# Half of x transposed by DMA, and a stricter order on VectorE, in a gated spectral and dense layer with its gradients

## The chip, the core and the metric

The kernel runs on one core of a Trainium2 chip. The metric is the device time of one launch in microseconds (us); the numbers below are medians of several runs, and the profile is one execution of the same program recorded by the hardware profiler.

## The reference

The forward pass mixes two branches with a gate, row by row. Branch A is a two-dimensional real Fourier transform of x, a product with a complex filter, and the transform back. Branch B is a dense layer with a squared ReLU between two products. The kernel returns the output and the gradients of A_x, A_w_r, A_w_i, w1, b1, w2, b2 and gate_w for a given grad_out.

```python
# S = 2048 rows, D = 1024, F = 3584, all bfloat16
x = A_x
g = sigmoid((x * gate_w).sum(-1, keepdims=True))
a = irfft2(rfft2(x) * (w_r + 1j * w_i))
h = relu(x @ w1 + b1); b = (h * h) @ w2 + b2
out = g * a + (1 - g) * b
# outputs: out, and the vjp of it for (A_x, A_w_r, A_w_i, B_w1, B_b1, B_w2, B_b2, gate_w)
```

Both branches take x = A_x; the input B_x is not used.

## The kernel before

The program has one main stream of TensorE work and one side stream. The main stream has four stages: the products of the dense layer forward and back (`mlp_in`), the gradient of w2 and then of w1 (`mlp_grads`, with blocks multiplied by a scheme of seven products instead of eight, which needs sums and differences of operands on VectorE), and the output and the gradient of x (`mlp_out`). The side stream is the Fourier branch; `spread` draws units of it between the units of the main stream, in proportion to the weight that each main unit yields.

The products need x and the scaled gradient with their columns on the partitions: xT and dbT. Both are made by TensorE from tiles of 128 rows. A tile takes eight 128 x 128 transposes into one of two PSUM buffers, and one copy to SBUF:

```python
def turn_tile(dst, i, src, copy, tie=None):
    pt = tps.tile([P, DC, P], BF16, name="pt", tag="tr", bufs=2)
    for b in range(DC):                                   # DC = 8
        later["turned"] = nc.tensor.transpose(pt[:, b, :], src[:, b * P : (b + 1) * P], identb[:])
        after(later["turned"], tie, mybir.DependencyClass.NoSync)
    copy(out=dst[:, :, of_tile(i)], in_=pt[:])

def weigh(i, src):                                        # row sum of x * gate_w, for the gate
    unused = f1.tile([P, 2, H], FDT, name="uv", tag="uv", bufs=2)
    weighed = nc.vector.tensor_tensor_reduce(... in0=src[:], in1=gwb[:], ..., accum_out=gsum[:, i : i + 1])
    after(weighed, later.get("b1"), mybir.DependencyClass.NoSync)

def gate(i0):                                             # gate of four tiles, then the gradient's rows scaled
    c_ = slice(i0, i0 + 4)
    nc.scalar.activation(omg[:, c_], gsum[:, c_], ACT.Sigmoid, scale=-1.0)
    nc.scalar.activation(gcol[:, c_], gsum[:, c_], ACT.Sigmoid)
    for i in range(i0, i0 + 4):
        later["scaled"] = nc.vector.tensor_scalar(out=dbn[:, i, :], in0=dbn[:, i, :], scalar1=omg[:, i : i + 1], ...)
```

`after(a, b, NoSync)` only fixes that a stands after b; it adds no semaphore between engines. The program is ordered by a scheduler within such bounds. `queued` ties each load to the one before it, so that the loads stand in one order on SyncE's queue:

```python
def turn_x(i):
    src = rows.pop(i)
    weigh(i, src)
    turn_tile(xT, i, src, nc.vector.tensor_copy if i == 1 else nc.scalar.copy, ...)

def turn_grad(i):
    turn_tile(dbT, i, dbn[:, i, :], nc.vector.tensor_copy, later["product"])

# ... (start: loads, tiles 0 to 3 turned and weighed, gate(0), rows_of_grad(1))
rows_of_x(2); rows_of_grad(2); rows_of_x(3); rows_of_grad(3)      # loads of four tiles each
before = {1: [4], 2: [5], 3: [6, 7], **{u: [u - 4] for u in range(12, 20)}}
grads_before = {**{u: [u - 4] for u in range(4, 12)}, **{u: [u - 12] for u in range(20, 28)}}
for u in range(32):
    for i in before.get(u, ()):
        turn_x(i)
    for i in grads_before.get(u, ()):
        turn_grad(i)
    next(units)                                           # eight matmuls of 128 x 512
    if u in (3, 15, 19):
        gate({3: 4, 15: 8, 19: 12}[u])
    if u == 17:
        for n in range(3):
            xs[n] = source(n, x_perm)                     # rows for the Fourier side
        stage = first_stage_of_x()
    if u > 19 and u % 2:
        next(stage)
```

Of these 32 units, 0 to 7 multiply xT's tiles 0 to 7 with w1 (results ph), 8 to 15 multiply dbT's tiles 0 to 7 with the transposed w2 (results pd); 16 to 23 and 24 to 31 do the same with the tiles 8 to 15. Within each eight, the first four units use the first four of those tiles. The transposed w2 (w2T) comes from DMAs that transpose (`turned`), two of 256 rows x 1024 for each group; units 8 to 15 need the first group.

A block of the gradient of w1 runs in steps: p1 and p2 (no sums needed), p4 of the block before, p6, p3 of the block before, p5, p7. p5 needs the sum 1 of its group, p6 sum 2, p7 sum 3, p4 sum 4. Each group serves two blocks. The additions (`add`) take a result from PSUM (pV) and a kept one:

```python
# class Turned(Block), for the gradient of w1
def add(self, t_, h, kept):
    turn["DVE"] = super().add(t_, h, kept)
    return turn["DVE"]

# mlp_grads, at the switch from the gradient of w2 to that of w1 (cut)
c.p1(); yield each
c.p2(); yield each
sums_of_x(3, tie=c.first)
b.p5()
sums_of_group(FG, 4, 3)
fetch(FG + 2, 0); yield each
b.p6(); yield each
# ... c.p5, c.p6 with sums_of_x(4), b.p7
c.p7()
sums_of_group(FG + 1, 1, 2, tie=c.added); yield each
b.p4(); yield each
b.p3(); yield each
for k in range(NB // 2 + 2, NB):
    g, second = divmod(k, 2)
    b = Turned(k)
    b.p1(); yield each
    # ... p2, a.p4 (and sums_of_group(g, 3, 4) for the first block of a group), p6, a.p3, p5
    b.p7()
    if second and g + 1 < len(jobs):
        sums_of_group(g + 1, 1, 2, tie=b.added)
    yield each
```

`in_turn(ins, "DVE")` sets an instruction after the last one recorded in turn["DVE"]; the folds of the Fourier side's last stage use it already.

Of the kernel before, what the change touches and what calls it, by code (L numbers as in the profile page):

```python
# [14 lines left out]
ALU = mybir.AluOpType  # L15
# [125 lines left out]
def kernel(  # L141
# [22 lines left out]
    nc = tc.nc  # L164
# [6 lines left out]
    g = Geo(S, D, F)  # L171
    S2, DC, FC = g.S2, g.DC, g.FC
    R1, R2 = g.R1, g.R2
    NT = S // P
    Q, H, LW, W1 = D // 4, D // 2, g.Df + 1, g.Df
    FGW, FG, FGC = g.FGW, g.FG, g.FGC
# [4 lines left out]
    turned = lambda out, in_: nc.sync.dma_start(out=out, in_=in_, transpose=True)  # L181
    ld, st = nc.sync.dma_start, nc.gpsimd.dma_start
    V, mm = nc.vector.tensor_tensor, nc.tensor.matmul
# [5 lines left out]
    x_perm = xf.rearrange("(p t) d -> t p d", t=S2)  # L189
# [41 lines left out]
    def of_tile(i):  # L231
        return slice(P * i, P * (i + 1))

    def after(ins, earlier, wait=mybir.DependencyClass.Sync):

        if earlier is not None:
            info = mybir.DependencyInfo(wait, mybir.DependencyReason.DATA)
            tc.add_manual_dep(ins.ins, earlier.ins.name, info, reason="paced")


    turn = {"PE": None, "DVE": None, "ACT": None, "copy": None}
# [5 lines left out]
    def in_turn(ins, eng):  # L247
        after(ins, turn[eng], mybir.DependencyClass.NoSync)
# [366 lines left out]
    def rows_of_w2(t_, fc, half, tie=None):  # L615
        src = B_w2[fc * P : (fc + 4) * P, half * H : (half + 1) * H]
        after(ld(out=t_[:, fc : fc + 4, :], in_=src.rearrange("(q p) e -> p q e", p=P)), tie)
# [4 lines left out]
    xT = xT_p.tile([P, DC, S], BF16, name="xT", tag="xT")  # L622
    dbT = xT_p.tile([P, DC, S], BF16, name="dbT", tag="dbT")

    later = {}
# [5 lines left out]
    def queued(ins):  # L631
        after(ins, later.get("row"), mybir.DependencyClass.NoSync)
        later["row"] = ins
# [9 lines left out]
    def turn_tile(dst, i, src, copy, tie=None):  # L643

        pt = tps.tile([P, DC, P], BF16, name="pt", tag="tr", bufs=2)
        for b in range(DC):
            later["turned"] = nc.tensor.transpose(pt[:, b, :], src[:, b * P : (b + 1) * P], identb[:])
            after(later["turned"], tie, mybir.DependencyClass.NoSync)
        copy(out=dst[:, :, of_tile(i)], in_=pt[:])  # L649

    def vectors(vrow):
        vps = tps.tile([P, FC], BF16, name="vps", tag="tr", bufs=2)
# [8 lines left out]
        nc.scalar.copy(out=gwb[:], in_=pb[:])  # L661
        return gwb

    def weigh(i, src):
        unused = f1.tile([P, 2, H], FDT, name="uv", tag="uv", bufs=2)
        weighed = nc.vector.tensor_tensor_reduce(
            out=unused[:].rearrange("p a b -> p (a b)"), in0=src[:], in1=gwb[:], scale=1.0, scalar=0.0,
            op0=ALU.mult, op1=ALU.add, accum_out=gsum[:, i : i + 1],
        )
        after(weighed, later.get("b1"), mybir.DependencyClass.NoSync)  # L670

    def gate(i0):

        c_ = slice(i0, i0 + 4)
        nc.scalar.activation(omg[:, c_], gsum[:, c_], ACT.Sigmoid, scale=-1.0)
        nc.scalar.activation(gcol[:, c_], gsum[:, c_], ACT.Sigmoid)
        for i in range(i0, i0 + 4):
            later["scaled"] = nc.vector.tensor_scalar(out=dbn[:, i, :], in0=dbn[:, i, :], scalar1=omg[:, i : i + 1], scalar2=None, op0=ALU.mult)

    def first_stage_of_x():  # L680
        f, ft = {0: folds(f1, xs[0], later["last"])}, {}
        for i in range(NT + 1):
            if i + 3 < NT:
                xs[i + 3] = source(i + 3, x_perm, later["last"])
            if i < NT:
                ft[i] = row_stage(f1, f[i], kf[:], later["last"])
                yield
            if i > 0:
                first_columns(f1, cf, 0, i - 1, ft[i - 1], later["last"])
            if i + 1 < NT:  # L690
                f[i + 1] = folds(f1, xs[i + 1], later["last"])
            yield
# [149 lines left out]
    def mlp_grads():  # L842
# [12 lines left out]
        jobs = [(h2T_scr, fg) for fg in range(FG)] + [(dhT_scr, fg) for fg in range(FG)]  # L855
# [34 lines left out]
        T_, S_, blk = {}, {}, {}  # L890
# [32 lines left out]
        class Block:  # L923
# [7 lines left out]
            def operands(self):  # L931
                (a11, a12), (_, a22) = quads(grp[self.g], FH)
                self.A = {"11": a11, "12": a12, "22": a22, **S_.setdefault(self.g, {})}
                self.S, self.T = S_[self.g], T_
                self.a11, self.a12, self.a22 = a11, a12, a22
                self.b11, self.b21, self.b22 = b11, b21, b22
# [19 lines left out]
            def add(self, t_, h, kept):  # L956
                return V(out=self.side(t_, h), in0=self.flat(self.V[:]), in1=self.flat(kept[:]), op=ALU.add)
# [36 lines left out]
        class Turned(Block):  # L994

            def operands(self):
                (self.a11, self.a12), (_, self.a22) = quads(xr, H)
                (self.b11, self.b21), (_, self.b22) = quads(grp[self.g], FH)
                self.S, self.T = X_, T_[self.g]

            flat = staticmethod(lambda ap: ap.rearrange("p (j f) -> p j f", j=2))

# [3 lines left out]
                return t_  # L1006

            def add(self, t_, h, kept):
                turn["DVE"] = super().add(t_, h, kept)
                return turn["DVE"]  # L1010

            def side(self, t_, h):
                return t_.rearrange("p (j h f) -> p h j f", j=2, h=2)[:, h]
# [18 lines left out]
        X_ = {}  # L1032
# [20 lines left out]
        def sums_of_group(g, *which, tie=None):  # L1053
            (g11, g21), (g12, g22) = quads(grp[g], FH)
            made = T_.setdefault(g, {})
            for n in which:
                if n == 3:
                    made[3] = fp16(g12)
                else:
                    tag = {1: "S3", 2: "S2", 4: "S4"}[n]  # L1060
                    made[n] = sb.tile([P, KH, FH], FP16, name=f"G{n}", tag=tag, bufs=2 if n == 1 else 1)[:]
                x, y = {
                    1: lambda: (g12, g11),
                    2: lambda: (g22, made[1]),
                    3: lambda: (g22, g12),
                    4: lambda: (g21, made[2]),
                }[n]()
                after(V(out=made[n], in0=x, in1=y, op=ALU.subtract), tie, mybir.DependencyClass.NoSync)

        NB = 2 * len(jobs)  # L1070
        each, none = 0.5, 1e-6
        for k in range(2):
            blk[k] = Block(k)
        fetch(1, 0, 1)
# [35 lines left out]
        for k in range(2, NB // 2):  # L1110
            a = blk.pop(k - 1)
            g, second = divmod(k, 2)
            b = blk[k] = Block(k)
# [35 lines left out]
        b, c = (Turned(NB // 2 + n) for n in range(2))  # L1149
# [10 lines left out]
        fetch(FG + 1, 1)  # L1160
        yield each
        c.p1()
        yield each
        c.p2()
        yield each
        sums_of_x(3, tie=c.first)
        b.p5()
        sums_of_group(FG, 4, 3)
        fetch(FG + 2, 0)
        yield each  # L1170
        b.p6()
        yield each
        c.p5()
        yield each
        c.p6()
        sums_of_x(4)
        yield each
        b.p7()
        yield each
        c.p7()  # L1180
        sums_of_group(FG + 1, 1, 2, tie=c.added)
        yield each
        b.p4()
        yield each
# [3 lines left out]
        for k in range(NB // 2 + 2, NB):  # L1188
            g, second = divmod(k, 2)
            b = Turned(k)  # L1190
            b.p1()
            yield each
            b.p2()
            if second:
                fetch(g + 2, 0)
            yield each
            a.p4()
            if not second:
                sums_of_group(g, 3, 4)
            yield each  # L1200
            b.p6()
            yield each
            a.p3()
            if not second:
                fetch(g + 1, 1)
            yield each
            b.p5()
            yield each
            b.p7()
            if second and g + 1 < len(jobs):  # L1210
                sums_of_group(g + 1, 1, 2, tie=b.added)
            yield each
            n = k - NB // 2 - 2
            if n < FC // 4:
                rows_of_w2(later["w2L"], 4 * n, 0, b.added)
            a = b
# [456 lines left out]
    rows = {}  # L1673

    def rows_of_x(k):
        for i in range(4 * k, 4 * (k + 1)):
            rows[i] = source(i, x_perm, None, "xsrc")

    def rows_of_grad(k):
        for i in range(4 * k, 4 * (k + 1)):  # L1680
            queued(ld(out=dbn[:, i, :], in_=go_perm[i]))

    def turn_x(i):
        src = rows.pop(i)
        weigh(i, src)
        turn_tile(xT, i, src, nc.vector.tensor_copy if i == 1 else nc.scalar.copy, later["gate_row"] if i == 2 else later.get("product"))

    def turn_grad(i):
        turn_tile(dbT, i, dbn[:, i, :], nc.vector.tensor_copy, later["product"])
# [32 lines left out]
    gate(0)  # L1722
    next(units)
    rows_of_grad(1)
    rows_of_x(2)
    rows_of_grad(2)
    rows_of_x(3)
    rows_of_grad(3)
    for t_, n in ((kf, "kf"), (flip, "flip"), (sel, "sel"), (cf, "cf")):
        after(st(out=t_[:], in_=cten[n].ap()), later["scaled"])  # L1730
    stage = None
# [2 lines left out]
# [3 lines that stand above are left out]
        for i in grads_before.get(u, ()):  # L1737
            turn_grad(i)
        next(units)
        if u in (3, 15, 19):  # L1740
            gate({3: 4, 15: 8, 19: 12}[u])
        if u == 17:
            for n in range(3):
                xs[n] = source(n, x_perm)
# [3 lines that stand above are left out]
# [97 lines left out]
```

## Time and profile before

Three runs took 1213.85, 1214.64 and 1214.91 us; the median is 1214.64. The profiled execution spans 1213.9 us at a mean granted TensorE clock of 0.997. Its stages, by start of their first work:

| stage | from us | what fills it |
|---|---|---|
| start, and 32 units with transposes between | 0 | TensorE, loads |
| rest of the products forward and back | 86 | TensorE |
| gradient of w2 | 466 | TensorE, VectorE |
| gradient of w1 | 641 | TensorE, VectorE |
| output, gradient of x | 845 | TensorE |

Of TensorE's work, the lines that the change speaks of, in the page's form (line engine op, out<-in, xcount | busy us, mean ns of one | idle us before, releaser):

```profile
L647 PE MATMUL pt<-identb,dbn 128*128 128x128 bf16 x128 | 10.2, 223 | 2.4 <-DVE dbT L649 2.4
L647 PE MATMUL pt<-identb,xsrc 128*128 128x128 bf16 x128 | 10.1, 231 | 0.0
```

The busy time of a group counts overlapping instructions once, so 128 transposes of 231 ns each fill 10.1 us. Names used below: xsrc are rows of x, dbn rows of grad_out (scaled in place), ph and pd results of the two products, wlo and whi outputs of a gradient block, G the sums of a group, pki and rf the Fourier side's last stage and its folded input. PE is TensorE, DVE VectorE, ACT ScalarE, SP SyncE.

### The profile page before, as it was taken

How to read it: one execution, taken by the hardware profiler on the slowest of the kernel's cores; microseconds unless marked ns; L12 is line 12 of the kernel's file. 1: busy time of each engine (PE TensorE's matmuls, PEld its weight loads, DVE VectorE, ACT ScalarE, POOL GpSimd, SP SyncE). 2: the span in 40 equal slices, each digit the busy share in tenths (PEclk: the TensorE clock that was granted, in tenths of full speed). 3: DMA queues.
4: the chain of work that ended last, by engine and by line, in shares of the span. 5: the costliest groups of instructions: out<-in, count | busy, mean ns of one | idle time of the engine just before them, and what ended most of it. 6: DMA issues, size and time to landing. Idle time of an engine off the chain costs nothing. (4 is left out here: it accounts for less than half of the span.)

```text
span 1213.9 us, 19997 instructions
## 1 busy us (share of the span) xinstructions
PE 1192.4 (98%) x7213; PEld 651.6 (54%) x7213; DVE 844.2 (70%) x1841; ACT 624.5 (51%) x1130; POOL 364.4 (30%) x587
## 2 busy tenths in 40 slices
PE   8999999999999999999999999999999999999998
PEld 4555545544444444444447888888444444444444
DVE  6756646676879887877789746765488866966464
ACT  5447757855877863444444435554455523233322
POOL 1024424423455551433333444444232100000000
PEclk9999999999999999999999999999999999999999
DMA  9647576575858598999999699867885699975551
GB/s 291 195 148 182 164 203 194 151 173 178 203 173 210 183 227 168 184 212 222 226 200 189 159 227 223 209 165 204 256 234 158 195 209 238 236 215 177 154 154 35
DMA packets 332656, 234.43 MB, mean 193 GB/s; under 512 B 197789, under 2 KB 291515, under 8 KB 332556
## 3 DMA queue, kind: packets, MB, share of 16 engines
q1 hardware_dynamic: 301104, 141.98, 52.1%
q0 software_dynamic: 30224, 90.61, 23.5%
q8 instruction: 56, 0.92, 0.3%
q10 hardware_dynamic: 1228, 0.57, 0.2%
q14 instruction: 44, 0.36, 0.1%
HBM read 107.24 MB, written 81.81 MB: 156 GB/s over the span
## 5 line engine op out<-in xcount | busy, mean ns | idle before, releaser
L746 PE MATMUL ph<-xT,w1g 128*128 128x512 bf16 x896 | 218.8, 379 | 1.6 <-ACT xT L649 1.6
L754 PE MATMUL pd<-dbT,w2T 128*128 128x512 bf16 x896 | 213.6, 381 | 1.9 <-DVE dbT L649 1.9
L754 PEld LDWEIGHTS <-w2T 128*128 128x128 bf16 x896 | 87.2, 98 | 104.7 <-issue 3.4
L746 PEld LDWEIGHTS <-w1g 128*128 128x128 bf16 x896 | 85.1, 98 | 93.0 <-DMA w1g<-in_B_w_dram 1.5
L758 DVE SCALAR_TENSOR_TENSOR dhT<-pd,rT 128x512 bf16<-128x512 f32 x108 | 74.2, 687 | 77.3 <-PE pd L754 62.8
L747 ACT ACTIVATE rT<-ph,b1col 128x512 bf16<-128x512 f32 x108 | 74.5, 690 | 47.2 <-PE ph L746 46.9
L1020 PEld LDWEIGHTS <-res 128*128 128x128 bf16 (+1 forms) x896 | 86.7, 98 | 13.8 <-issue 2.8
L1372 PEld LDWEIGHTS <-dS 128*128 128x128 f16 x588 | 57.1, 98 | 66.8 <-issue 1.2
L226 POOL DMA_DIRECT2D r<-y_scr x96 | 58.3, 612 | 108.4 <-ACT re L553 42.4
L419 ACT CAST x<-px 64x512 f16<-64x512 f32 x128 | 74.2, 579 | 28.5 <-PE px L416 27.4
L226 POOL DMA_DIRECT2D z_scr<-u x96 | 58.6, 617 | 92.0 <-ACT u L294 48.0
L1020 PEld LDWEIGHTS <-X 128*128 128x128 f16 x672 | 64.9, 98 | 8.7 <-issue 0.9
L748 ACT ACTIVATE h2T<-rT 128x512 bf16<-128x512 bf16 x108 | 68.0, 630 | 2.2
L1372 PEld LDWEIGHTS <-odd 128*128 128x128 bf16 (+1 forms) x392 | 38.1, 98 | 44.9
L1372 PEld LDWEIGHTS <-even 128*128 128x128 bf16 (+1 forms) x392 | 38.0, 98 | 44.4
L456 POOL DMA_DIRECT2D y_scr<-pc x64 | 36.0, 564 | 69.0 <-DVE pc L453 66.2
L946 PEld LDWEIGHTS <-S 128*128 128x128 f16 x336 | 32.8, 98 | 39.7 <-DVE S L920 0.3
L394 POOL COPY w<-wn 128x512 bf16<-128x512 bf16 x32 | 23.1, 721 | 84.3 <-DVE tt L427 66.3
L568 ACT CAST rt<-pki 128x1024 f16<-128x1024 f32 x32 | 32.4, 1012 | 28.5 <-PE pki L566 28.2
L1394 DVE TENSOR_TENSOR cu<-pV,u 128x512 f16<-128x512 f32 x27 | 18.6, 689 | 40.8 <-PE pV L1372 35.1
L1345 POOL DMA_DIRECT2D out_dram<-gxo x14 | 7.6, 541 | 130.7 <-DVE gxo L1344 130.7
L1372 PE MATMUL pX<-wT,dS 128*128 128x512 f16 x196 | 44.8, 379 | 0.5 <-DVE dS L1368 0.5
(275 smaller groups left out, 2483.3 us busy)
## 6 DMA issues: line engine op xcount, KB each, us to landing
h2T_scr<-h2T POOLq DMA_DIRECT2D x28, 512.0 KB, 4.1
dhT_scr<-dhT POOLq DMA_DIRECT2D x28, 512.0 KB, 5.7
z<-z_scr SPq DMA_DIRECT2D x64, 128.0 KB, 3.0
y_scr<-pc POOLq DMA_DIRECT2D x64, 128.0 KB, 4.5
ax_scr<-yo POOLq DMA_DIRECT2D x32, 256.0 KB, 4.1
out_dram<-whi POOLq DMA_DIRECT2D x28, 256.0 KB, 4.4
out_dram<-wlo POOLq DMA_DIRECT2D x28, 256.0 KB, 4.4
even<-h2T_scr SPq DMA_DIRECT2D x8, 896.0 KB, 6.3
```

Source lines behind the costliest of these rows:

```text
L226: issue(out=a, in_=b) if stored else issue(out=b, in_=a)
L419: nc.scalar.copy(out=x[lanes[n], c, :, 0:HW], in_=px[lanes[c], n])
L456: st(out=y_scr[:][c, :, :, h].rearrange("r x t l -> (r x) t l"), in_=pc[:, n])
L568: nc.scalar.copy(out=rt[n][:], in_=pk[:])
L746: opened(mm(ph[:], lhsT=w1g[:, dc, fc % 2 * P : (fc % 2 + 1) * P], rhs=xT[:, dc, ss], start=(dc == 0), stop=(dc == DC - 1)), fc)
L747: nc.scalar.activation(rT[:], ph[:], ACT.Relu, bias=b1col[:, fc : fc + 1])
L748: nc.scalar.activation(h2T, rT[:], ACT.Square)
L754: opened(mm(pd[:], lhsT=w_[:, ec, fc % FGC * P : (fc % FGC + 1) * P], rhs=dbT[:, ec, ss], start=(ec == 0), stop=(ec == DC - 1),), fc)
L758: return STT(out=dhT, in0=pd[:], scalar=2.0, in1=rT[:], op0=ALU.mult, op1=ALU.mult, accum_out=gb1part[:, fc, sb : sb + 1],)
L946: self.mm = mm(acc[:], lhsT=lhs[:, t, c_], rhs=rhs[:, t, :], start=start and t == 0, stop=t == KH - 1, skip_group_check=True,)
L1020: ins = mm(acc[:, j * FH : (j + 1) * FH], lhsT=lhs[:, t, c_], rhs=rhs[:, t, :], start=start and first_ is None, stop=t == KH - 1, skip_gro ...
L1372: pe(mm(acc[:], lhsT=lhs[:, c, :], rhs=rhs[:, c, :], start=start and c == 0, stop=c == KH - 1, skip_group_check=True,))
```

## The change

The change has several parts. Tiles 8 to 15 of x are transposed by eight loads with a transpose, directly into xT, while their plain rows are still loaded for the row sums; TensorE's transposes and ScalarE's copies for them go. At the start the copies of transposes come first on VectorE: tile 3's copy moves to VectorE, the row sums 0 to 3 come after it, later row sums and the scaling of the gradient's rows stand behind the latest copy, and the scaling of rows 4 to 7 moves from unit 3 to unit 6. In the gradient of w1, sums of a group and additions stand in one order on VectorE, and the sums 1 and 2 come after the first chain of the group's own first block. At the switch five steps weigh 0.25 instead of 0.5, so that less of the side stream falls there.

```diff
-        copy(out=dst[:, :, of_tile(i)], in_=pt[:])
+        later["copied"] = copy(out=dst[:, :, of_tile(i)], in_=pt[:])
@@ weigh
-        after(weighed, later.get("b1"), mybir.DependencyClass.NoSync)
+        after(weighed, tie, mybir.DependencyClass.NoSync)
@@ gate
             later["scaled"] = nc.vector.tensor_scalar(out=dbn[:, i, :], ...)
+            after(later["scaled"], later["copied"], mybir.DependencyClass.NoSync)
@@ class Turned
-                self.S, self.T = X_, T_[self.g]
+                self.S, self.T = X_, T_.setdefault(self.g, {})
             def add(self, t_, h, kept):
-                turn["DVE"] = super().add(t_, h, kept)
-                return turn["DVE"]
+                ins = super().add(t_, h, kept)
+                in_turn(ins, "DVE")
+                turn["DVE"] = ins
+                return ins
@@ sums_of_group
-                after(V(out=made[n], in0=x, in1=y, op=ALU.subtract), tie, mybir.DependencyClass.NoSync)
+                ins = V(out=made[n], in0=x, in1=y, op=ALU.subtract)
+                after(ins, tie, mybir.DependencyClass.NoSync)
+                if g > FG:
+                    in_turn(ins, "DVE")
+                    turn["DVE"] = ins
@@ the switch
-        each, none = 0.5, 1e-6
+        each, slow, none = 0.5, 0.25, 1e-6
   (the yields after c.p1, c.p2, the fetch after b.p5, b.p6, c.p5: "yield slow" for "yield each";
    five such lines)
         c.p7()
-        sums_of_group(FG + 1, 1, 2, tie=c.added)
@@ the blocks after it
             b.p1()
+            if not second:
+                sums_of_group(g, 1, 2)
             yield each
   ...
             b.p7()
-            if second and g + 1 < len(jobs):
-                sums_of_group(g + 1, 1, 2, tie=b.added)
             yield each
@@ turn_x
-        src = rows.pop(i)
-        weigh(i, src)
-        turn_tile(xT, i, src, nc.vector.tensor_copy if i == 1 else nc.scalar.copy, ...)
+        if i >= NT // 2:
+            weigh(i, rows.pop(i), later["copied"])
+            return
+        turn_tile(xT, i, rows[i], nc.vector.tensor_copy if i in (1, 3) else nc.scalar.copy, ...)
+        if i >= 3:
+            for n in range(4 if i == 3 else 1):
+                weigh(n if i == 3 else i, rows.pop(n if i == 3 else i), later["copied"] if i == 3 else None)
@@ the loads
-    rows_of_x(2)
-    rows_of_grad(2)
-    rows_of_x(3)
-    rows_of_grad(3)
+    for k in (2, 3):
+        for i in range(4 * k, 4 * (k + 1)):
+            queued(turned(xT[:, :, of_tile(i)], x_perm[i]))
+        rows_of_x(k)
+        rows_of_grad(k)
@@ the units
-        if u in (3, 15, 19):
-            gate({3: 4, 15: 8, 19: 12}[u])
+        if u in (6, 15, 19):
+            gate({6: 4, 15: 8, 19: 12}[u])
```

More of the change, by code (lines that the diff above doesn't have):

```diff
@@ L662, in everywhere, with weigh @@
         return gwb
-    def weigh(i, src):
+    def weigh(i, src, tie):
         unused = f1.tile([P, 2, H], FDT, name="uv", tag="uv", bufs=2)
@@ L1162, in mlp_grads @@
         c.p1()
-        yield each
+        yield slow
         c.p2()
-        yield each
+        yield slow
         sums_of_x(3, tie=c.first)
@@ L1169, in mlp_grads @@
         fetch(FG + 2, 0)
-        yield each
+        yield slow
         b.p6()
-        yield each
+        yield slow
         c.p5()
-        yield each
+        yield slow
         c.p6()
@@ L1683, in turn_x @@
     def turn_x(i):
-        src = rows.pop(i)
-        weigh(i, src)
-        turn_tile(xT, i, src, nc.vector.tensor_copy if i == 1 else nc.scalar.copy, later["gate_row"] if i == 2 else later.get("product"))
+        if i >= NT // 2:
+            weigh(i, rows.pop(i), later["copied"])
+            return
+        turn_tile(xT, i, rows[i], nc.vector.tensor_copy if i in (1, 3) else nc.scalar.copy, later["gate_row"] if i == 2 else later.get("product"))
+        if i >= 3:
+            for n in range(4 if i == 3 else 1):
+                weigh(n if i == 3 else i, rows.pop(n if i == 3 else i), later["copied"] if i == 3 else None)
     def turn_grad(i):
```

## The prediction

> **What bounds the kernel now.** I read the engines' busy shares first, then the stretches of the span, then the waits of TensorE alone, and last the timeline around the two stretches in which TensorE idles and which the change touches.
>
> The page's first part gives busy us, share of the span and instructions:
>
> ```profile
> PE 1192.4 (98%) x7213; PEld 651.6 (54%) x7213; DVE 844.2 (70%) x1841; ACT 624.5 (51%) x1130; POOL 364.4 (30%) x587
> ```
>
> TensorE is busy for 1192.4 of 1213.9 us. So a gain can come from two sources only: TensorE work that disappears, and the 21.5 us in which TensorE is idle. A perfect removal of all idle time would be 1.8%. The stretches show where these 21.5 us lie (columns: length, busy us and count of PE, PEld, DVE, ACT, POOL, then granted clock, DMA share, GB/s):
>
> ```profile
> 25.00:37.00 12.00, 7.64 (x46) 3.94 (x44) 11.60 (x23) 2.82 (x6) 1.46 (x2) 0.86 1.05 387
> 37.00:52.00 15.00, 15.00 (x113) 8.50 (x111) 11.15 (x27) 4.35 (x6) 0.71 (x1) 1.00 0.32 121
> 650.00:676.00 26.00, 23.23 (x203) 19.61 (x201) 25.18 (x41) 12.11 (x23) 12.38 (x19) 1.00 0.78 170
> 735.00:845.00 110.00, 108.37 (x1100) 96.91 (x1099) 69.89 (x216) 60.29 (x111) 50.88 (x83) 1.00 0.80 196
> 870.00:950.00 80.00, 77.26 (x447) 37.41 (x446) 69.68 (x150) 43.34 (x70) 20.54 (x35) 1.00 0.68 193
> ```
>
> TensorE idles 12.00 - 7.64 = 4.4 us at 25 to 37 us, 2.8 us at the switch from the gradient of w2 to that of w1 (650 to 676), 1.6 us in the gradient of w1, and 2.7 us in the last stage, which the change does not touch. In the first two VectorE is full (11.60 of 12.00, 25.18 of 26.00). TensorE's list of waits names what ended its idle time:
>
> ```profile
> PE pt L647 <- DVE dbT L649: 2.4, 1, 2.4
> PE pV L1020 <- DVE wlo L957: 2.0, 1, 2.0
> PE pd L754 <- DVE dbT L649: 1.9, 1, 1.9
> ```
>
> All three are copies or additions of VectorE that had come late. The timeline of 23 to 33 us shows why (start, length, instruction):
>
> ```profile
> 23.45 1.08 DVE L678 TENSOR_SCALAR dbn<-dbn,omg 128x1024 bf16<-128x1024 bf16 x2 [2.35 <-DMA dbn<-in_grad_out_dram]
> ...
> 26.19 1.22 DVE L666 CUSTOM_DVE_ANT_0 uv<-xsrc,gwb 128x1024 f16<-128x1024 bf16 x1
> ...
> 27.34 0.68 DVE L649 COPY dbT<-pt 128x1024 bf16<-128x1024 bf16 x1
> ...
> 28.08 0.61 PE L647 MATMUL pt<-identb,dbn 128*128 128x128 bf16 x8 [2.42 <-DVE dbT L649]
> ...
> 32.81 3.29 PE L754 MATMUL pd<-dbT,w2T 128*128 128x512 bf16 x8 [1.95 <-DVE dbT L649]
> ```
>
> VectorE sits at the scaling of the gradient, which waits 2.35 us for a load, then does a row sum of x (1.22 us), and only then the copy of a finished transpose at 27.34. TensorE can't go on because both banks for transposes are full.
>
> [...] the copy at 27.34 stands behind a scaling that waits for data. [...] after two gaps of 2.42 and 1.95 us, with little between them, the granted clock was 0.86 over 25 to 37 us, and the eight products at 32.81 took 3.29 us where eight take 1.89. [...] at 15 to 20 us, when the transposing loads of w2T are nearly all that moves, the DMA share is 0.90 at 155 GB/s, and at 55 to 60 us, with such loads again, 218 GB/s at a share of 1.22. [...]
>
> **Part 1: half of x's transposes leave TensorE.** Eight tiles with eight transposes each go. A transpose's own duration (231 ns) overstates it, since they are pipelined. At 45.35 and 47.52 us two products of eight matmuls start 2.17 us apart with one tile's transposes between them; without any (645.46, 647.18, 648.91) they are 1.73 apart. So a tile costs 2.17 - 1.73 = 0.44 us, and eight cost 3.5 us, in a stretch where TensorE is full (37 to 70 us). ScalarE also loses eight copies of 1.01 us, off the path. **-3.5 us.**
>
> **Part 2: order on VectorE at the start.** Row sums 8 to 15 now stand behind the latest copy, so the one at 26.19 is no longer ahead of the copy of dbT. The second scaling moves from after unit 3 to after unit 6 and also stands behind a copy. What is to be won is the two gaps and the slow restart: 2.42 + 1.95 + (3.29 - 1.89) + 0.32 for the eight transposes after it (0.93 instead of 0.61) = 6.1 us. Rows 4 to 7 of the gradient land by about 25.4 either way, and without the row sum the fourth copy would be done near 27, about when unit 7 ends, so I take the whole 6.1. The copy of tile 3 on VectorE beside that of tile 2 on ScalarE would bring the first product from 9.99 to about 9.2, but tile 4's transposes wait for a load until 11.80 just after it, so I count only 0.3. **-6.4 us.**
>
> **Part 3: the new loads.** Two megabytes more have to come, at 155 to 218 GB/s: 9 to 13 us of DMA. Before, the DMA engines are full until 40 us (share 1.05 at 25 to 37) and almost idle from 40 to 52 us. So the last loads should land about 12 us later, near 52. There is a second limit. SyncE took 7.41 us to issue the two transposing loads of w2T, 1 MB in all. Eight of 256 KB would take 8 x 7.41 / 4 = 14.8 us, an estimate by size, and this queue issues in order. Its last gradient row, issued before by 33.2, would be issued near 48. Unit 16 started at 51.87 and unit 20 at 60.56; less 6.4 and four or eight tiles of 0.44 they start near 44 and 50.6. The half of xT that unit 16 needs is issued by about 29: safe. The other, for unit 20, is issued by about 41 and takes 5 to 11 us, as w2T's loads do: barely in time. The last scaling (unit 19, about 49) and the first rows of the Fourier side would wait on VectorE for loads that land at 52 to 55, with the copies of dbT behind them again. I set 2.3 us for this, between nothing and one more stall of the kind seen. **+2.3 us.**
>
> **Part 4: the switch.** Of 2.6 us (1.98 and 0.64), the larger wait is for the addition at 672.36, which stood behind three sums of group 8 (668.29, 669.76, 671.23, each 1.22) and two of the side stream. Two of these three now come after the next block's first chain, and all are in one order with the additions. Five steps draw half as much side work. Of the side stream some 64 units are left for a weight of 48 in this stage (counted in the code, with the 24 kept for the last one), so 5 x 0.25 x 64 / 48 = 1.7 units are put off, with 1.7 us or so of VectorE work each: 3 us less in a stretch of 26 where it is full. I take 2.2 of the 2.6. **-2.2 us.**
>
> **Part 5: one order in the gradient of w1.** 1.6 us of small waits lie there, mostly for folds of the Fourier side that stand behind sums of a group. The sums stay as long and come one chain later. I take **-0.4 us**. The side work put off, about two units, comes where the last stage already waits for VectorE: **+0.6 us.**
>
> Sum: -3.5 - 6.4 + 2.3 - 2.2 - 0.4 + 0.6 = -9.6, so 1214.64 - 9.6 = 1205.0 us. The stages between are full on TensorE (25.00 of 25.00 us in nearly every stretch from 275 to 650), so what is won early should reach the end.
>
> **Rivals.** (a) *The loads become the wait.* If the eight transposing loads run slower than by size, or w2T's next load is held behind them, xT comes late at unit 20 and TensorE stands for 5 to 10 us, with a slow restart on top: 1210 to 1218. For it speak 155 GB/s and the in-order queue; against it the empty stretch from 40 to 52 us. (b) *Only the transposes count.* The wait of VectorE at 23.45 is one for data, so the copies may just stand behind the scaling again, and the switch may find another sum in the way. Then only 3.5 us and a little of the rest remain: about 1210. For it speaks that two megabytes more are asked for; against it, that the needed gradient rows are issued before them. (c) *The strict order costs.* An addition that waits for a chain holds up the folds behind it, in each of twelve blocks: 0.3 us each would be +3.6 in place of -0.4: about 1209. (d) *All goes well:* no new wait and both stretches cleared, 1214.64 - 3.5 - 6.4 - 2.6 - 1.6, about 1200.
>
> **Range and chances.** From (d) and a little below to the mild end of (a): 1199 to 1213. A gain over 2% would need 24.3 us, more than all idle time: 0.01. A loss over 2% would need 24 us of new waits, several stalls of the first stretch: 0.02. Within 2%: 0.97.
>
> **What would show it.** Part 1: 64 transposes from xsrc instead of 128, and units 16 to 19 about 1.73 us apart. Part 2: no TensorE wait for dbT at 25 to 33 us, a clock of 1.00 there, and the first pd product near 27.5. Part 3: DMA busy at 40 to 52 us; a TensorE wait for xT, or for dbT behind a scaling, near 50 to 60 us would be (a). Part 4: no wait for wlo in the 26 us of the switch. Part 5: waits of pki for rf that shrink, or, under (c), grow. The prediction is wrong if the product stage ends less than 5 us earlier, or if what it wins is gone again at the end.

## The result, and the profile after

Four runs of the changed kernel have a median of 1207.67 us (1206.89 to 1208.85), against 1214.78 for the kernel before beside them. The ratio is 0.9938, 95% interval 0.9919 to 0.9957: 7.1 us faster by the medians. The profiled execution is the fastest of the four and spans 1205.1 us.

The three views shown before, for the changed kernel. The page's busy shares:

```profile
PE 1182.8 (98%) x7055; PEld 647.7 (54%) x7149; DVE 845.4 (70%) x1842; ACT 614.4 (51%) x1121; POOL 365.5 (30%) x587
```

The stretches (columns as before):

```profile
25.00:37.00 12.00, 11.95 (x86) 6.63 (x85) 7.75 (x17) 2.63 (x4) 1.54 (x2) 1.00 1.03 292
37.00:52.00 15.00, 14.89 (x75) 7.04 (x76) 10.97 (x25) 3.62 (x7) 1.42 (x2) 1.00 1.05 284
52.00:70.00 18.00, 13.40 (x92) 7.19 (x92) 11.38 (x29) 8.65 (x20) 1.42 (x2) 0.91 0.95 258
650.00:676.00 26.00, 26.00 (x232) 22.44 (x231) 24.41 (x39) 12.50 (x23) 10.26 (x18) 1.00 0.80 146
735.00:845.00 110.00, 108.35 (x1068) 93.71 (x1067) 69.21 (x211) 58.15 (x110) 49.71 (x80) 1.00 0.92 201
870.00:950.00 80.00, 77.50 (x452) 38.75 (x458) 71.13 (x153) 42.19 (x69) 21.62 (x37) 1.00 0.71 201
```

And TensorE's two longest waits (us in total, times, longest):

```profile
PE ph L747 <- ACT rT L748: 4.5, 1, 4.5
PE pki L566 <- DVE rf L558: 1.9, 4, 0.7
```

The stretch at 25 to 37 us is cured: TensorE is busy for 11.95 of 12.00 us instead of 7.64, at a clock of 1.00 instead of 0.86. So is the switch, 26.00 of 26.00. The DMA engines, at a share of 0.32 over 37 to 52 us before, are full (1.05). A new hole stands at 52 to 70 us, 13.40 of 18.00, with the clock at 0.91, and TensorE's longest wait is now one for ScalarE.

The timeline of that hole, TensorE, ScalarE and VectorE together (start, length, instruction):

```profile
48.85 1.23 DVE L666 CUSTOM_DVE_ANT_0 uv<-xsrc,gwb 128x1024 f16<-128x1024 bf16 x1 [3.83 <-DMA xsrc<-in_A_x_dram]
...
50.45 1.89 PE L747 MATMUL ph<-xT,w1g 128*128 128x512 bf16 x7
...
53.55 0.21 ACT L675 ACTIVATE omg<-gsum 128x4 f32<-128x4 f32 x1 [4.39 <-DVE gsum L666]
...
55.70 0.42 DVE L256 TENSOR_TENSOR uv<-src 128x512 f16<-128x512 bf16 x1 [2.19 <-DMA src<-in_A_x_dram]
...
56.50 0.20 ACT L263 COPY f<-uv 128x2 f16<-128x2 f16 x1 [2.13 <-DVE uv L257]
56.60 0.68 ACT L748 ACTIVATE rT<-ph,b1col 128x512 bf16<-128x512 f32 x1
...
57.33 3.57 PE L747 MATMUL ph<-xT,w1g 128*128 128x512 bf16 x8 [4.55 <-ACT rT L748]
...
57.97 0.68 DVE L649 COPY dbT<-pt 128x1024 bf16<-128x1024 bf16 x1
...
61.63 1.89 PE L747 MATMUL ph<-xT,w1g 128*128 128x512 bf16 x8
```

VectorE waits 3.83 us for the first late rows of x (tile 12), makes four row sums, then waits 2.19 us for the first rows of the Fourier side. ScalarE stands behind it twice: at the sigmoid of those sums (4.39 us), and at a copy of that fold (2.13). The relu of a finished product (56.60) comes after both, and TensorE's next product, unit 21 at 57.33, waits 4.55 us for it; the copy of dbT, at 57.97, is late as well. Unit 20 started at 50.45, and unit 22 at 61.63. Without the hole unit 22 would have started at 50.45 + 0.44 + 1.73 + 0.44 + 1.73 + 0.44 (two tiles of transposes and one set of eight from the Fourier side at 0.44 each, two products) = 55.2. So the hole costs 6.4 us: 4.6 of idle time, and the rest a slow restart, the eight products taking 3.57 us instead of 1.89.

To place the gains I read four landmarks in each trace: the first ph product after the 32 units, the first product of the gradient of w2, that of w1, and that of the last stage. Times in us from the span's start:

| kernel | after 32 units | gradient of w2 | gradient of w1 | last stage | span |
|---|---|---|---|---|---|
| before | 86.27 | 465.58 | 641.53 | 844.75 | 1213.9 |
| changed | 82.54 | 461.71 | 637.67 | 837.56 | 1205.1 |
| changed, all transposes on TensorE (run 1) | 80.34 | 459.61 | 635.57 | 835.15 | 1204.7 |
| before, transposing loads only (run 2) | 91.37 | 470.81 | 646.77 | 851.47 | 1220.2 |
| before, gradient of w1 only (run 3) | 86.09 | 465.26 | 641.21 | 840.79 | 1211.7 |
| late rows, four side units (run 4) | 75.69 | 457.25 | 638.21 | 838.98 | 1209.9 |
| late rows, six side units (run 5) | 77.13 | 456.31 | 632.26 | 831.85 | 1199.5 |
| before, VectorE order at the start only (run 6) | 80.21 | 459.49 | 635.44 | 838.91 | 1207.5 |
| changed, only tiles 8 to 11 by DMA (run 8) | 78.25 | 457.51 | 633.46 | 841.04 | 1209.3 |
| changed, transposes both ways (run 9) | 83.89 | 463.16 | 639.11 | 838.54 | 1208.4 |
| before, smaller weights only (run 10) | 85.16 | 464.33 | 640.29 | 841.79 | 1210.3 |
| before, order in the gradient of w1 only (run 11) | 85.22 | 464.40 | 640.35 | 840.77 | 1211.5 |

The change wins 3.7 us by the first landmark and keeps it to the third; the gradient of w1 takes 199.9 us instead of 203.2 and adds 3.3.

A landmark comes from one execution. Four traces have the start of the kernel before (before, runs 3, 10 and 11), and their first landmarks lie at 86.27, 86.09, 85.16 and 85.22 us. Run 10 shows where most of that comes from. It has the same two gaps as before, 2.46 and 1.95 us, but not the slow restart:

```profile
28.65 0.61 PE L647 MATMUL pt<-identb,dbn 128*128 128x128 bf16 x8 [2.46 <-DVE dbT L649]
...
33.38 1.89 PE L754 MATMUL pd<-dbT,w2T 128*128 128x512 bf16 x8 [1.95 <-DVE dbT L649]
```

The eight products take 1.89 us here and 3.29 in the trace of before. So a difference of about 1 us at the first landmark can be chance.

### The profile page after: what moved, and what is told of

Same layout as the page of the kernel before. It is cut to its first block, busy times and chain, and to the rows that moved or that the text cites. A ratio compares the mean times of both kernels' runs of the same rounds, so it can differ in the third digit from the quotient of the medians.

```text
span 1205.1 us, 19779 instructions
## 1 busy us (share of the span) xinstructions
PE 1182.8 (98%) x7055; PEld 647.7 (54%) x7149; DVE 845.4 (70%) x1842; ACT 614.4 (51%) x1121; POOL 365.5 (30%) x587
## 4 chain that ended last, share of the span: by engine, by line
PE 88%; DVE 4%; DMA 4%; ACT 2%; issue 1%; POOL 0%; SPq 0%; ACTq 0%; DVEq 0%
PE pd L755 15%; PE ph L747 15%; PE pX L1378 13%; PE pV L1378 10%; PE pX L947 8%; PE pX L1023 6%; PE pV L947 6%; PE pV L1023 5%; PE acc L1475 2%; PE pu L310 2%; PE pk L277 1%; PE px L416 1%; DMA xsrc<-in_A_x_dram 1%; DMA r<-y_scr 1%; PE pv L447 1%
## 5 line engine op out<-in xcount | busy, mean ns | idle before, releaser
L747 PE MATMUL ph<-xT,w1g 128*128 128x512 bf16 x867 | 216.0, 381 | 7.3 <-ACT rT L748 4.5
L755 PE MATMUL pd<-dbT,w2T 128*128 128x512 bf16 x876 | 209.5, 379 | 0.9
L810 POOL DMA_DIRECT2D h2T_scr<-h2T x28 | 20.7, 740 | 75.5 <-ACT h2T L749 42.0
```

The lines of the kernel that those rows point to most:

```text
L747: opened(mm(ph[:], lhsT=w1g[:, dc, fc % 2 * P : (fc % 2 + 1) * P], rhs=xT[:, dc, ss], start=(dc == 0), stop=(dc == DC - 1)), fc)
L755: opened(mm(pd[:], lhsT=w_[:, ec, fc % FGC * P : (fc % FGC + 1) * P], rhs=dbT[:, ec, ss], start=(ec == 0), stop=(ec == DC - 1),), fc)
```

## The experiments

My theory: the start's new VectorE order and the gradient's new order are gains, while the transposing loads lose more by the hole than they save on TensorE. The rival: the loads are a gain, and the hole comes from something else.

**Run 1: all transposes on TensorE again.** In the changed kernel, the loads of the kernel before and

```diff
         if i >= NT // 2:
-            weigh(i, rows.pop(i), later["copied"])
+            tie = later["copied"]
+            turn_tile(xT, i, rows[i], nc.scalar.copy, later.get("product"))
+            weigh(i, rows.pop(i), tie)
             return
```

> The changed kernel with the tiles 8 to 15 of x transposed on TensorE again and no transposing loads of x. Theory A (the eight loads cost more than they save: they take 3.5 us off TensorE and bring a stall of 6.4 us at unit 21, because VectorE and ScalarE stand in order behind rows that land late): 3 us faster than the changed kernel, about 1204.8, and no wait of TensorE between 45 and 65 us. Rival B (the stall has another source, such as the order of the row sums, and the loads are a gain): 3.5 us slower than the changed kernel, about 1211, with the stall still there.

Measured: 1204.85 us, ratio to before 0.9926 (0.9914 to 0.9939), and no hole. TensorE's stretches at 37 to 52 and 52 to 70 us:

```profile
37.00:52.00 15.00, 15.00 (x112) 8.42 (x110) 14.04 (x34) 9.43 (x13) 1.42 (x2) 1.00 0.54 185
52.00:70.00 18.00, 18.00 (x144) 10.62 (x143) 10.38 (x26) 11.30 (x24) 1.43 (x2) 1.00 0.76 184
```

Theory A holds: each of the five runs is faster than each of the changed kernel, and the hole is gone. The transposing loads cost 2.8 us by the medians and 2.2 by the first landmark. By the ratios to before it is only 1.5, with intervals that overlap, so the size is less sure than the sign.

**Run 2: the transposing loads alone**, on the kernel before: its `weigh` stays, tiles 8 to 15 return before `turn_tile`, and the loads are those of the change.

> The kernel before with nothing but the transposing loads of the tiles 8 to 15 in place of TensorE's transposes. Theory A: -3.5 us of TensorE work and a stall of about 5 to 7 us near 50 to 60 us, beside the old stall at 25 to 33 us: 1 to 3 us slower than before, about 1216 to 1218. Rival B (the loads are a gain by themselves): 1211.

Measured: 1221.86 us, ratio 1.0057 (1.0044 to 1.0070). The sign is theory A's; the size, 8.0 us by the medians, is larger. Its longest wait shows why:

```profile
PE pd L754 <- DVE dbT L649: 9.4, 2, 6.0
```

The old hole at the start grows (TensorE is busy for 0.00 of 5.00 us at 30 to 35), and a second one comes at 45 to 50 us (1.64 of 5.00). VectorE, for which TensorE waits, is itself busy for only 2.21 and 2.78 us there. My reading, from the order in the program, is that the row sums 8 to 11, which stand ahead of copies, now wait for rows behind the transposing loads. So the start's new order isn't a mere extra: without it the loads lose far more than in the changed kernel.

**Run 3: the gradient of w1 alone**, order and weights of the change, the start as before.

> The kernel before with the new order and the smaller weights in the gradient of w1 alone, the start as before. From the two traces this stage is 3.3 us shorter. Theory A: -3.3 us, about 1211.4, if the work put off costs nothing later. Rival C (the side work put off has to be done in the last stage and half of it comes back): -1.5 to -2 us, about 1213.

Measured: 1210.87 us, ratio 0.9969 (0.9955 to 0.9983), 3.0 us by the medians, near theory A. The stage is 199.6 us long instead of 203.2. The last stage took 370.9 us in this trace and 369.2 in that of before, but it also took 367.5 to 370.9 in the other traces of the table, so a price for the side work put off can't be told from scatter.

**Run 4: the late rows used later**, in the changed kernel, its loads untouched:

```diff
-    before = {1: [4], 2: [5], 3: [6, 7], **{u: [u - 4] for u in range(12, 20)}}
+    before = {1: [4], 2: [5], 3: [6, 7], **{u: [u - 4] for u in range(12, 16)}, **{u: [u - 8] for u in range(20, 24)}}
-        if u in (6, 15, 19):
-            gate({6: 4, 15: 8, 19: 12}[u])
-        if u == 17:
+        if u in (6, 15, 23):
+            gate({6: 4, 15: 8, 23: 12}[u])
+        if u == 21:
-        if u > 19 and u % 2:
+        if u > 23 and u % 2:
```

> The changed kernel with the row sums 12 to 15 at units 20 to 23 instead of 16 to 19, the scaling of rows 12 to 15 at unit 23 instead of 19, and the first folds of the Fourier side at unit 21 instead of 17. The loads stay as they are. Theory A (the stall is one of order: VectorE stands at a row sum and at a fold whose rows land at 48.8 and 55.7 us, and the copies of dbT and ScalarE's relu stand behind them): most of the 6.4 us goes, 1201 to 1203. Rival D (TensorE would wait for the loads anyway, for xT or for dbn): 1206 to 1208, with a wait of TensorE for xT or dbT between 45 and 65 us.

Measured: 1211.67 us, ratio 0.9981 (0.9968 to 0.9993): neither expectation came. The hole was gone (75.69 at the first landmark instead of 82.54, of which a part is two side units fewer). But against the changed kernel 2.4 us were given back by the start of the gradient of w2, 5.0 in that gradient, 0.9 in the next and 3.4 in the last stage. The 5.0 us are, but for 0.1, two waits at the start of the gradient of w2:

```profile
PE pV L947 <- DVE even L921: 3.2, 1, 3.2
PE pX L947 <- DVE S L921: 1.6, 1, 1.6
```

The VectorE timeline there:

```profile
459.48 0.70 DVE L426 TENSOR_TENSOR tt<-x,w 128x1028 f16<-128x1028 f16 x1 [2.12 <-ACT x L419]
460.09 0.68 DVE L453 TENSOR_TENSOR pc<-pv,vc 128x512 f16<-128x512 f32 x1
460.69 0.68 DVE L454 TENSOR_TENSOR pc<-pv,vc 128x512 f16<-128x512 f32 x1
461.29 0.69 DVE L427 TENSOR_TENSOR tt<-x,w 128x1028 f16<-128x1028 f16 x1
461.89 2.28 DVE L895 TENSOR_TENSOR T<-dbn 128x4096 f16<-128x4096 bf16 x1
464.10 1.66 DVE L921 TENSOR_TENSOR S<-even 128x2048 f16<-128x2048 bf16 x1
```

Four operations of the side stream, the first of which waits for ScalarE, stand ahead of the gradient's first sums; in the changed kernel none does. My edit had drawn four side units instead of six among the 32 units, so the stream stood two units further back at this point. The smaller losses were not traced.

**Run 5: the same with six side units**, `if u > 22 and (u % 2 or u == 24)`.

> As the run with the row sums, scaling and folds later, but with six side units drawn among the 32 units, as in the changed kernel, instead of four. Theory A (what that run gave back at the start of the gradient of w2 was the side stream standing two units further back, so that four operations of it fell ahead of the first sums on VectorE): the 4.9 us wait at 460 to 472 us goes and the time is 1201 to 1203. Rival (the start simply comes too early for those sums, whatever the side stream does): the wait stays, about 1207 to 1211.

Measured: 1201.41 us (1201.29 to 1202.02), ratio 0.9886 (0.9865 to 0.9907). This beats both kernels, by 13.4 us against before. No wait for the sums is left, so theory A holds. The stretches of the old hole read:

```profile
37.00:52.00 15.00, 14.89 (x75) 7.11 (x76) 10.41 (x26) 5.57 (x10) 1.42 (x2) 1.00 1.08 275
52.00:70.00 18.00, 17.55 (x140) 10.22 (x140) 15.24 (x37) 8.37 (x18) 1.42 (x2) 1.00 1.10 288
```

The DMA engines are at least as full as in the changed kernel (1.08 and 1.10), and TensorE idles for 0.6 us in these 33. VectorE still waits for the rows of tile 12, about as long and as late as in the changed kernel:

```profile
49.16 1.23 DVE L666 CUSTOM_DVE_ANT_0 uv<-xsrc,gwb 128x1024 f16<-128x1024 bf16 x1 [3.77 <-DMA xsrc<-in_A_x_dram]
```

But now only one row sum stands there, and nothing that TensorE needs is held up by it. So the late rows alone don't make the hole; the order of what stands behind them does. Row sums, scaling and folds were moved together, so it isn't shown which of them counts most. Against run 1, which has no hole either, this run is 3.2 us earlier at the first landmark and 3.4 faster by the medians (the intervals of the ratios don't overlap); that is what the DMA transposes save.

**Run 6: the VectorE order at the start alone**, transposes on TensorE, gradient of w1 as before.

> The kernel before with the new order of VectorE at the start alone: no transposing loads of x, the gradient of w1 as before. Theory A: the two waits for dbT and the slow restart go, -6.4 us, about 1207.5. Rival (part of the gain needs the gradient's new order or is taken back at a later stage): 1209 to 1211.

Measured: 1209.59 us, ratio 0.9953 (0.9935 to 0.9971), 5.3 us by the medians and 6.1 at the first landmark. The total lies in the rival's range, but not for the rival's reason: the lead is 6.1 us at the next two landmarks too, so that nothing is taken back later. Both waits for dbT are gone, as theory A had it. What theory A had too large is the slow restart, which not every execution of the kernel before has: against the trace of run 10, which has none, the first landmark is only 5.0 us earlier.

**Run 7: plain rows 8 to 15 from GpSimd's queue.** In the changed kernel, x and gradient rows from 8 on are issued by `nc.gpsimd.dma_start` in one order of their own.

> The changed kernel with the plain rows 8 to 15 of x and of the gradient loaded from GpSimd's queue, the transposing loads staying on SyncE's. Theory S (SyncE's queue, 2 us for each transposing load, is what makes the rows late): the rows land before 45 us, the stall goes, 1201 to 1203. Rival W (the 16 DMA engines are full, share 1.05 to 50 us, so that the rows land as late whoever issues them): 1206 to 1208 and a stall of 4 us or more between 45 and 65 us.

Measured: 1236.62 us, ratio 1.0166 (1.0134 to 1.0197): neither expectation came. The plain rows started at 10.65 us, beside the transposing loads of w2T instead of behind them, and what followed on SyncE's queue slowed: 27.94 us instead of 7.42 for w2T's two loads, 3.77 instead of 2.01 for four rows of the gradient, 29.20 instead of 16.35 for xT's eight. SyncE's queue in this run:

```profile
11.57 27.94 SPq L181 DMA_TRANSPOSE w2T<-in_B_w_dram  x2
39.56 3.77 SPq L1691 DMA_DIRECT2D dbn<-in_grad_out_dram  x4
43.37 29.20 SPq L181 DMA_TRANSPOSE xT<-in_A_x_dram  x8
```

and in the changed kernel:

```profile
11.57 7.42 SPq L181 DMA_TRANSPOSE w2T<-in_B_w_dram  x2
...
21.08 7.85 SPq L181 DMA_TRANSPOSE xT<-in_A_x_dram  x4
```

Between 20 and 55 us the DMA engines moved 144 GB/s at a share of 1.22 in this run, and 305 GB/s at 1.05 in the changed kernel. So the time that SyncE spends on a transposing load is no fixed cost of the instruction: the same two loads took 7.42 us and 27.94. Rows 4 to 7 of the gradient came behind them: VectorE waited 31.14 us for the first, and TensorE once for 28.5 us. Whether the queue or the engines held up the rows in the changed kernel isn't decided by this run, since it also moved the rows in time.

**Run 8: only tiles 8 to 11 by DMA**, 12 to 15 on TensorE as in run 1.

> The changed kernel with only the tiles 8 to 11 of x transposed by DMA and 12 to 15 on TensorE. The queue is 8.5 us shorter ahead of the last rows, and 1 MB less has to come. Theory A (the stall comes from the last rows' lateness): no stall, and 4 x 0.44 = 1.8 us less than with all transposes on TensorE (1204.85), so about 1203. Rival (the stall starts with the first transposing loads): about 1208 to 1209, with a stall of 4 us or more.

Measured: 1203.45 us, ratio 0.9912 (0.9887 to 0.9936), as theory A had it. The gain over run 1 is 1.4 us by the medians, which is within noise, but 2.1 at the first landmark (78.25 against 80.34), for 1.8 expected. Five of its six runs lie at 1202.7 to 1205.0 and one at 1211.1; the trace is of this slowest run, and it has no hole at the start but a wait of 4.9 us of pki for rf near 780 us, in a part that this edit doesn't touch.

**Run 9: transposes of x by DMA and on TensorE too.** Run 1 with the loads of the change kept; the copies overwrite what the loads wrote.

> The changed kernel with the eight transposing loads kept and the same tiles transposed on TensorE as well (the copies overwrite what the loads wrote). So TensorE has all its 128 transposes of x again and the DMA engines have the extra 2 MB too. Theory F (the stall ends at a fixed moment, when the late rows have landed, near 57 us; work taken off TensorE ahead of it only makes the wait longer): the 3.5 us of transposes fill part of the wait, which shrinks from 4.5 to about 1 us, and the time is that of the changed kernel, 1207 to 1209. Rival G (the stall has a fixed length, whatever TensorE does before it): 3.5 us slower than the changed kernel, about 1211.

Measured: 1210.63 us, ratio 0.9959 (0.9946 to 0.9972), which is near rival G; the first landmark is 83.89, 1.35 us after the changed kernel's. But TensorE's wait is another one now:

```profile
PE pt L647 <- DMA xsrc<-in_A_x_dram: 3.7, 3, 2.9
```

The transposes themselves wait for the late plain rows. So this run doesn't settle whether the hole's end is fixed in time. It shows that the extra loads, with nothing saved, cost 3.5 us at the first landmark against run 1, in a wait for late rows.

**Runs 10 and 11: the switch's weights alone, and the order in the gradient of w1 alone**, on the kernel before.

> The kernel before with the five smaller weights at the switch alone. Theory A (the order is what removes the 2.6 us of waits, the weights only put side work off): under 1 us faster than before. Rival H (room on VectorE is what counts): 2.5 to 3 us faster.

> The kernel before with the new order of sums and additions in the gradient of w1 alone, the weights all 0.5. Theory A: 2 to 3 us faster than before, no wait of TensorE for wlo at the switch. Rival H: the wait for wlo or another one stays, and less than 1 us is won.

Measured: weights 1214.09 us, ratio 0.9984 (0.9970 to 0.9998), order 1212.48, ratio 0.9976 (0.9963 to 0.9990). The stage takes 201.5 us with the weights, 200.4 with the order, 199.6 with both (run 3), 203.2 with neither. With the weights alone the old wait stays, `PE pV L1020 <- DVE wlo L957` for 1.8 us. With the order alone it is gone and another stands there:

```profile
PE pX L1022 <- DVE G L1070: 1.3, 1, 1.3
```

Now a chain waits for a sum that the strict order put late. In run 3, with both, neither wait is left. By the times, the order brings most of it: 2.2 us by the medians against 0.6 for the weights, which is theory A. The stage lengths have 2.8 and 1.7 of 3.6 us for both, so the two overlap. What the weights add to the order (0.8 us of the stage) isn't clear of noise.

## Why the prediction was right, and where it wasn't

The prediction was 1205.0 us in a range of 1199 to 1213, and the median is 1207.67. The number alone shows little: about 1209 and 1210 of rivals (c) and (b) lie nearer. The runs show that the gains came from where the prediction put them, and that one cost, part 3, was far too small. The prediction had named a sign for this: it is wrong if the product stage ends less than 5 us earlier. That stage ended 3.9 us earlier (461.71 instead of 465.58), so its account of the start as a whole failed, by the term of the new loads.

- **Part 1, -3.5.** -3.2 (run 5 against run 1 at the first landmark). The spacing of two products, not a transpose's own 231 ns, gave it.
- **Part 2, -6.4.** -6.1 at the first landmark against the trace of before, -5.0 against that of run 10, -5.3 by the medians (run 6). The prediction counted the slow restart, 1.7 us, as a part of every execution, and run 10 hasn't got it. In the changed kernel the fourth copy starts at 25.98 us and the first pd product at 27.94, against the 27 (for the copy's end) and 27.5 that I had put down; no wait for dbT is left. The first product moved from 9.99 to 9.59 us only, as it then waited 1.02 us for w1.
- **Part 3, +2.3.** This is the step that was mis-sized: it cost 6.4 us by the trace, 5.4 by landmarks (82.54 against 77.13 in run 5). The loads came about when the working said: SyncE took 16.4 us for the eight transposing loads, for 14.8; VectorE's wait for the rows of tile 12 ended at 48.85 us and that for the first Fourier rows at 55.70, for loads "at 52 to 55". What I weighed wrongly was what such waits set off. I named the last scaling and the first Fourier rows; the row sum of tile 12 waited as well, and the scaling only stood behind the fold. I named the copies of dbT behind them, but not ScalarE, which waited 4.39 and 2.13 us for VectorE's sums and fold with its relu behind them. And I put less than one stall of the first kind for it all, though this one had a gap of 4.5 us and a slow restart. Rival (a) was near: TensorE stood for 4.5 us, where (a) had 5 to 10, but for ScalarE's relu and not for xT.
- **Part 4, -2.2, and part 5, -0.4.** Together -3.3 in the two traces of before and after, -3.0 by the medians of run 3. Most of it is the order's (runs 10 and 11). Rival (c), a strict order that costs 0.3 us a block, didn't come: all waits for folds in the changed kernel are 2.2 us, and 2.5 before.
- **The side work put off, +0.6.** Not seen: the last stage took 367.5 us after and 369.2 before, within its scatter.

By landmarks the start was to bring 7.6 us and brought 3.7; in the profiled executions the gradient of w1 and the last stage won 3.3 and 1.6 us, where a gain of 2.6 and a loss of 0.6 had been put down. These errors have opposite signs, and the 1.6 us are within scatter, so that the total came so near is in part luck.

Rival (b), that only the transposes count, is refuted: the two orders gain without them (runs 6 and 3), and alone with their loads they make the kernel slower (run 2).

## What to carry to other kernels

- Moving work from a full engine to idle DMA engines (share 0.32 at 37 to 52 us before, 1.05 after) can be paid for by whatever waits next in the queue. List each consumer of the loads that come later, and move those consumers (row sums, scaling, first folds) behind the work that doesn't need them. Here that turned a part that cost 2.2 us at the first landmark (run 1) into one that saves 3.2 (run 5).
- When an engine waits for data, follow the wait through the engines that wait for it: here 3.83 and 2.19 us on VectorE became 4.39 and 2.13 on ScalarE and 4.55 on TensorE. Count a slow restart as well as the gap, but as one that may or may not come: after nearly the same pair of gaps, eight products took 3.29 us in one trace and 1.89 in another.
- After shifting a stage, look at how the side stream meets the next change of stage: two side units fewer brought waits of 4.8 us some 380 us later.

## What the runs showed of the hardware that I had not expected

- Transposing loads next to plain loads of GpSimd's queue were slow in run 7: 144 GB/s at a DMA share of 1.22, against 305 GB/s with one queue in the changed kernel; the two loads of w2T kept SyncE for 27.94 us instead of 7.42. One run shows this, and its cause is open.
- In the changed kernel TensorE's gap of 4.55 us ended at 57.33, the granted clock was 0.73 over 55 to 60 us, and the eight products after the gap took 3.57 us, against 1.89 for others. In run 7, after gaps of 28.5 and 5.3 us, the granted clock was 0.50 over 60 to 65 us, and the eight products that started at 62.74 took 3.57 us as well.
- With shorter gaps the length alone didn't decide it. After the pair of 2.42 and 1.95 us the products of the kernel before were slow (3.29 us for eight), and after the pair of 2.46 and 1.95 in run 10 they weren't (1.89). After a gap of 3.23 us in run 4 eight took 1.90.
